# Handing out freed on-chip places in another order between two mixtures of a fused attention and two-mixture kernel

## The chip, the cores and the metric

The kernel runs on one core of one Trainium2 chip. The metric is the device time of one execution in microseconds (us), the median of several runs. Engines are named as the profile names them: PE (TensorE, matrix multiplies), DVE (VectorE), ACT (ScalarE), POOL (GpSimd) and SP (the sync engine, which issues all transfers here).

## The reference

```python
attn_out = _attn_ref(q, k, v)            # 4 x 8 heads x 576 x 64: pooled attention + local attention
x = attn_out.transpose(0, 2, 1, 3).reshape(2304, 512)
# first mixture, d_ff 2048
h = x @ w_in
x = (h * cos(h)) @ w_out
# second mixture, d_ff 1536
xn = x / sqrt(mean(x * x) + 1e-6) * rms_g
g = xn @ w_gate
out = (g * sigmoid(g) * (xn @ w_val)) @ w_out2
```

All is in fp32; the weights of both mixtures arrive as 64-bit words and are turned into fp32 on the chip.

## The kernel before, in words

The tokens are 9 tiles of 256. The first mixture takes tiles 0 to 4 one at a time, then 5 and 6 as a pair, then 7 and 8 as the last pair. For the last pair it walks over 16 slices of d_ff (units 0 to 15). Each unit is one product `h` (line 1004, 12 matmuls, w_in piece) and, once cos has been worked out, one product `y` (line 1070, 12 matmuls, w_out piece) that adds into four PSUM banks. They are called h0 to h15 and y0 to y15 here. Between h and y of a unit stand ACT (lines 1022, 1027, 1038) and DVE (1024, 1029, 1040; 1040 sometimes on POOL). A product in fp32 is made of three passes over a high and a low part, so each operand is split into a rounded part (ACT) and a remainder (DVE or POOL).

The second mixture has 12 weight slices c and three groups g of three token tiles. Its g and val products (line 1499, `gvp`, 36 steps n in the order of the list `CG`; the first steps are c = 0, 1, 2 with g = 0) are done by a seven-product scheme, so weights and tokens first need sums and differences. What each needs:

- A weight slice c: its fp32 pieces are loaded from a scratch array in HBM into a tile `wf` (line 1269, 512 KB), then DVE and POOL form four differences (`wt`, line 1339), ACT rounds (line 1353) and DVE or POOL form remainders (line 1355) into tiles `wc` and `wv`. This is called the split of slice c.
- A token tile t: it is normalised (`norm`: load `y2`, squares, a chain of eleven small DVE instructions on `nst`, a scaling at line 1422 or 1424, transposes `yt` on PE at line 1404), stored (line 1415) and loaded again (`yn`, line 1461); then sums `xs` (line 1468) and remainders `xc` (line 1478). The second half is called the comb of tile t. Tiles 7 and 8 skip the store and load.

All of these tiles live in 19 on-chip places `wa0` to `wa18` of 4 KB per partition. Seventeen of them hold w_in and w_out pieces of the first mixture; each comes free when the last pair has used its piece, and goes to the pool `lt`. The other two carried the second mixture's weights while they were still 64-bit words (staging); they go to the pool `wx` once the last word piece has been written to HBM. The function `late` takes places one after the other and hands them out as `y` (token tiles, two halves of the pair named y and s), `s` (sums, and the differences `wt` of a split), `wf`, or as parts of a weight set `W` (three `wc` and half a `wv`). Since `late` takes them strictly in the order that it lists, a place that is free can stay unused while `late` waits for an earlier one.

The order of instructions on each engine is fixed when the program is built, by a planner (class `Order`, line 55): generators ask for engines and places, and the planner always issues what could start first by its own table of costs. On the chip each engine then runs its list in order, and so does SP's queue of transfers: a transfer that waits for its place holds back all behind it.

```python
    def free_w(p):
        give("lt" if p[2] == "wa" else p[2], p)
```
```python
        yield wait(("wfs", C2 - 1))
        for _ in range(2):
            p = yield take("wa")
            give("wx", p)
```

Of the kernel before, what the change touches and what calls it, by code (L numbers as in the profile page):

```python
# [10 lines left out]
F32R = mybir.dt.float32r  # L11
# [14 lines left out]
NG = 3  # L26
GT, SW = NTILE // NG, TT // 2
C2 = DFF2 // 128
# [26 lines left out]
class Order:  # L55
# [20 lines left out]
    def give(self, name, item, t=None):  # L76
        self.pools.setdefault(name, []).append((self.now() if t is None else t, item))
# [4 lines left out]
    @staticmethod  # L82
    def wait(ev):
        return "wait", ev

    @staticmethod
    def take(name, rest=0):
        return "take", name, rest
# [103 lines left out]
def fused_kernel(ctx: ExitStack, tc, q, k, v, w_in, w_out, w_gate, w_val, w_out2, rms_g, mask, bmask, out):  # L192
# [3 lines left out]
    wait, take, give, done = S_.wait, S_.take, S_.give, S_.set  # L196
# [76 lines left out]
    W, WP = {}, {}  # L273
# [814 lines left out]
    def y_bank(j, y, yi, i, tag, x, t0):  # L1088
# [22 lines left out]
    us = dram.tile([C2, 128, NTILE, 2, SW], F32, name="us")  # L1111
    EARLY = 3
    EN, NE = 5, 4
    LATE1 = ("y", "s", "y", "s", "y", "s")
    LATE2 = ("wf", "wf")
    LATE = C2 - 3
    CG = [(c, g) for g in range(NG) for c in range(EARLY)] + [(c, g) for c in range(EARLY, LATE) for g in range(NG)] \
        + [(c, g) for g in range(NG) for c in range(LATE, C2)]
    SG = ((0, 1), (2, 3), (4, 5), (6, 7), (8,))
    C3 = C2 // 2  # L1120
    YB = (("y", "st"), ("y", "wo"))
# [1 line left out]
    def due2(n):  # L1123
        return T0 + T1 * NTILE + GU * n
# [7 lines left out]
    def second_mixture():  # L1132
# [19 lines left out]
        give("xc", pr.tile([128, 7, 2, 2, GT * SW], F32R, tag="xc0", name="xc"))  # L1152
        done("p2")
        S_.add(late(), 0.0)
        S_.add(w2_loads(), 0.0)
        for t in range(EN, NTILE):
# [18 lines left out]

    def late():
        yield wait("p2")
        for n in LATE1:
            p = yield take("lt")
            give(n, p)  # L1180
        v = []
        for x in range(3):
            w = []
            for _ in range(3):
                p = yield take("lt" if x == 0 else ("lt", "wx"))
                w.append(p[0].tile([128, 2, 4, 128], F32R, tag=p[1], name="wc"))
            if x < 2:
                p = yield take("lt" if x == 0 else ("lt", "wx"))
                v.append(p[0].tile([128, 2, 2, 2, 128], F32R, tag=p[1], name="wv"))
            w.append(v[x // 2][:, x % 2])  # L1190
            give("W", w)
            for n in LATE2 if x == 0 else ():
                p = yield take("lt")
                give(n, p)
    def y_last(j, y, yi):
        due = S_.cur["due"]
        t0 = (S_.cur["t"], "PE")
        ts = xs(T1S[j])[2]
        for t in ts:
            y_i = yield take("y")  # L1200
            s_i = yield take("s")
            st = yield take("nst")
            P2["yr", t] = y_i[0].tile([128, 2, DM], F32, tag=y_i[1], name="y2"), y_i, s_i[0].tile([128, 4, TT], F32, tag=s_i[1], name="yT"), s_i, st
        for i in range(len(yi)):
            S_.add(y_square(ts[i // 2], i % 2, y[i], i, yi[i], t0), due)
            S_.add(y_copy(ts[i // 2], i % 2, y[i], i, yi[i], t0), due)
# [54 lines left out]
    def w2_loads():  # L1261

        for c in range(C2):
            S_.due(due2(CG.index((c, 0))) - 40.0)
            x = yield take("wf")
# [54 lines left out]
    def splits():  # L1320
        for c in range(C2):
            d = due2(CG.index((c, 0))) - 20.0
            S_.due(d)
# [164 lines left out]
    def product(n, m, bank, first, at):  # L1488
        c, g = CG[n]
        x, k, part = MW[m]  # L1490
        yield wait(("sp", c, k))
        S_.due(due2(n) + GU / 7 * at)
        yield "PE", 1.05
        w = P2["W", c][k][:, :, 2 * part:2 * part + 2]
        xc = P2["xc", g]
        i = 0
        for kk in range(2):
            for a, b in ((0, 0), (0, 1), (1, 0)):
                PE.matmul(bank, w[:, a, kk], xc[:, x, b, kk], start=first and i == 0, stop=i == 5, skip_group_check=True)  # L1499
                i += 1  # L1500
# [6 lines left out]
    def products():  # L1507
        N = NG * C2
        for n in range(N + 1):
            d = due2(n) - EV  # L1510
            if n < N:
                c, g = CG[n]
                for j in range(GT):
# [20 lines left out]
            if n:  # L1534
                yield wait(("v2", n - 1))
                yield from product(n - 1, 3, p["e"][1], False, 11)
                S_.add(ev_p1(n - 1, p), d)
                pc, pg = CG[n - 1]
                if pg == NG - 1:
# [12 lines left out]
    def half(x):  # L1552
        return x[:, :GT * SW]
# [44 lines left out]
    def ev_p1(n, st):  # L1598
        yield from ev_add(st["e"][1], st["u2"], st["u2"], None)
        free_bank(st["e"][0])  # L1600
        yield wait(("sl", n))
        yield from ev_u(n, st["u2"], st["sl"], 0)

    def ev_u(n, v, sl, s):
# [3 lines left out]
        yield "SP", 0.6  # L1608
        c, g = CG[n]
        SP.dma_start(us[c, :, GT * g:GT * g + GT, s], half(v).rearrange("p (j w) -> p j w", j=GT))  # L1610
# [234 lines left out]
```

## Time and profile before

| what | value |
|---|---|
| time, median of 3 runs | 992.78 us (992.71 to 993.03) |
| the profiled execution | 994.65 us, of it 992.6 us from the first to the last instruction (the span) |
| PE busy | 956.1 us, 96% of the span |
| PE busy from 200 to 400 us, and from 620 to 900 us | 199.7 of 200 us, 279.9 of 280 us |
| DVE busy | 721.8 us, 73% |
| ACT busy | 543.7 us, 55% |
| POOL busy | 272.6 us, 27% |
| mean granted PE clock | 0.993 of full speed |

A row of a timeline gives the start, the length up to the end of its last instruction, the engine, the source line, the operation, what it writes and reads, and how often; in square brackets stands the idle time before it and what ended that. Since matmuls overlap at their ends, the cost of a group is best read from its start to the start of the next. Windows give the busy time of every engine in a stretch. All times are from the start of the span.

### The profile page before, as it was taken

To read this page: it belongs to the slowest core of one execution; us is meant where nothing else is said; L and a number is where in the kernel's file an instruction comes from. 1 tells how busy PE (TensorE), PEld (TensorE's weight loads), DVE (VectorE), ACT (ScalarE), POOL (GpSimd) and SP (SyncE) were. 2 spreads that over 40 slices of the span, in tenths; PEclk is the share of its full clock that TensorE was granted. 3 is DMA by queue.
4 is the path that set the end of the run, shared out by engine and by line. 5 is a ranking of instruction groups with operands and counts; after the bars stand their busy time and mean duration, and the time that the engine had idled before them with its cause. 6 is when DMAs were issued, how large, how long until landed. Compare 5 with 4: busy or idle time off the path is not lost.

```text
span 992.6 us, 19109 instructions
## 1 busy us (share of the span) xinstructions
PE 956.1 (96%) x7102; PEld 880.5 (89%) x7102; DVE 721.8 (73%) x1459; ACT 543.7 (55%) x1090; POOL 272.6 (27%) x326
## 2 busy tenths in 40 slices
PE   6888899999999999999999989999999999999998
PEld 6787788888988888788888878999999999999998
DVE  2789976587767675666584698587666688999895
ACT  3657985678587865647564555243222334544442
POOL 3867675444435311001050452000000014300000
PEclk9999999999999999999999999999999999999999
DMA  8788634567766653543231311232322144454432
GB/s 236 214 230 250 180 118 118 159 182 194 214 201 171 183 167 118 186 147 143 89 123 43 128 64 32 65 91 81 95 77 77 49 149 133 124 170 138 150 118 75
DMA packets 160333, 136.07 MB, mean 137 GB/s; under 512 B 72176, under 2 KB 133744, under 8 KB 160240
## 3 DMA queue, kind: packets, MB, share of 16 engines
q1 hardware_dynamic: 160240, 134.85, 45.1%
q8 instruction: 56, 0.92, 0.4%
q14 instruction: 37, 0.30, 0.1%
HBM read 98.64 MB, written 36.18 MB: 136 GB/s over the span
## 4 chain that ended last, share of the span: by engine, by line
PE 81%; DVE 6%; issue 3%; POOL 3%; SPq 3%; DMA 2%; ACT 2%; DVEq 0%; POOLq 0%; ACTq 0%
PE gvp L1499 26%; PE y L1070 18%; PE h L1004 17%; PE o L1752 13%; PE bav L745 2%; PE btr L641 1%; SPq L475 1%; PE avp L589 1%; POOL wwa L322 1%; PE yt L1404 1%; DVE xc L1478 1%; PE bs L684 1%; PE bat L720 1%; DMA pq<-in_q 1%; PE sps L534 1%
## 5 line engine op out<-in xcount | busy, mean ns | idle before, releaser
L1499 PE MATMUL gvp<-xc,wc 128*128 128x384 f32 x1296 | 232.9, 336 | 1.5 <-ACT tmp L1561 1.4
L1499 PEld LDWEIGHTS gvp<-xc,wc 128*128 128x128 f32 x1296 | 226.4, 189 | 2.4 <-ACT tmp L1561 1.7
L1570 DVE TENSOR_TENSOR tmp<-gvp,tmp 128x384 f32<-128x384 f32 x180 | 99.5, 554 | 58.1 <-PE gvp L1499 53.7
L1004 PE MATMUL h<-big,wwa 128*128 128x256 f32 (+1 forms) x756 | 125.5, 319 | 1.5 <-DVE t L1029 1.0
L1004 PEld LDWEIGHTS h<-big,wwa 128*128 128x128 f32 x756 | 108.7, 192 | 11.9 <-DVE t L1029 1.2
L1752 PE MATMUL o<-wo,wc 128*128 128x256 f32 x972 | 118.5, 280 | 0.1
L1752 PEld LDWEIGHTS o<-wo,wc 128*128 128x128 f32 x972 | 115.7, 190 | 0.3 <-DVE tmp L1776 0.3
L1070 PE MATMUL y<-wwa,big 128*128 128x512 f32 x432 | 110.0, 398 | 3.6 <-DVE big L1040 3.6
L1070 PEld LDWEIGHTS y<-wwa,big 128*128 128x128 f32 x432 | 78.7, 188 | 21.4 <-DVE big L1040 5.4
L1004 PE MATMUL h<-big,wwb 128*128 128x256 f32 (+1 forms) x504 | 84.8, 319 | 0.1
L1070 PE MATMUL y<-wwb,big 128*128 128x512 f32 x324 | 82.2, 398 | 1.1 <-POOL big L1040 1.1
L1024 DVE SCALAR_TENSOR_TENSOR t<-kk,h 128x512 f32<-128x512 int32 x72 | 48.9, 681 | 43.7 <-ACT kk L1022 43.5
L1004 PEld LDWEIGHTS h<-big,wwb 128*128 128x128 f32 x504 | 72.8, 192 | 7.7 <-issue 0.8
L1022 ACT ACTIVATE kk<-h 128x512 int32<-128x512 f32 x72 | 42.6, 591 | 55.4 <-PE h L1004 55.1
L1070 PEld LDWEIGHTS y<-wwb,big 128*128 128x128 f32 x324 | 59.0, 188 | 13.7 <-POOL big L1040 1.7
L1636 POOL TENSOR_TENSOR wt<-wo 128x256 f32<-128x256 f32 x10 | 9.8, 978 | 208.7 <-DVE wc L1355 183.4
L1029 DVE TENSOR_TENSOR t<-h,t 128x512 f32<-128x512 f32 x72 | 49.3, 686 | 20.0 <-ACT t L1027 19.6
L1038 ACT ACTIVATE big<-t 128x512 fp32r<-128x512 f32 x72 | 45.2, 628 | 29.9 <-DVE t L1029 28.7
L1027 ACT ACTIVATE t<-t,cst 128x512 f32<-128x512 f32 x72 | 51.8, 721 | 17.1 <-DVE t L1024 16.7
L1561 ACT ACTIVATE tmp<-gvp 128x384 f32<-128x384 f32 x36 | 17.7, 491 | 78.1 <-PE gvp L1499 77.9
L1695 ACT ACTIVATE wc<-ut 128x512 fp32r<-128x512 f32 (+1 forms) x60 | 34.2, 584 | 44.2 <-DVE ut L1681 27.5
L1040 DVE TENSOR_TENSOR big<-t,big 128x512 fp32r<-128x512 f32 x56 | 42.9, 767 | 19.0 <-ACT big L1038 18.8
(184 smaller groups left out, 1738.3 us busy)
## 6 DMA issues: line engine op xcount, KB each, us to landing
us<-tmp SPq DMA_DIRECT2D x72, 192.0 KB, 2.0
uf<-us SPq DMA_DIRECT2D x48, 256.0 KB, 2.9
rawwa<-in_moe_w_out SPq DMA_DIRECT2D x21, 512.0 KB, 4.4
wfs<-rawwa SPq DMA_DIRECT2D x36, 256.0 KB, 2.5
rawwa<-in_moe_w_gate SPq DMA_DIRECT2D x12, 512.0 KB, 4.0
rawwa<-in_moe_w_val SPq DMA_DIRECT2D x12, 512.0 KB, 4.6
wf<-wfs SPq DMA_DIRECT2D x12, 512.0 KB, 4.0
vb<-in_v SPq DMA_DIRECT2D x80, 64.0 KB, 2.9
```

What stands on the lines that cost most here:

```text
L1004: PE.matmul(h[:, w_ * ci:w_ * ci + w_], a[:, ksl], x_at(x, kk), start=m == 0, stop=m == 11)
L1022: ACT.activation(out=kk, in_=h, func=ACTF.Copy, scale=INV2PI, bias=0.25)
L1024: DVE.scalar_tensor_tensor(out=t, in0=kk, scalar=TWOPI, in1=h, op0=ALU.mult, op1=ALU.subtract)
L1027: ACT.activation(out=t, in_=t, func=ACTF.Sin, scale=-1.0, bias=cst[:, 0:1])
L1029: DVE.tensor_tensor(out=t, in0=h, in1=t, op=ALU.mult)
L1038: ACT.activation(out=gh, in_=t, func=ACTF.Copy)
L1040: (POOL if e == "POOL" else DVE).tensor_tensor(out=gl, in0=t, in1=gh, op=ALU.subtract)
L1070: PE.matmul(y[j][b], g[:, tsl], a, start=(first and ci == 0 and i == 0), stop=(last and c == 15 and i == 2))
L1499: PE.matmul(bank, w[:, a, kk], xc[:, x, b, kk], start=first and i == 0, stop=i == 5, skip_group_check=True)
L1570: DVE.tensor_tensor(out=half(o), in0=a, in1=half(b), op=ALU.add)
L1695: ACT.activation(out=o[:, 0], in_=src, func=ACTF.Copy)
L1752: PE.matmul(b[m][1][:, l], u[0][x][:, j, l], w[:, y, k], start=(p == 0 and l == 0 and i == 0), stop=(p == C3 - 1 and i == 2), skip_group_c ...
```

## The change

`late` gets one list instead of two. Before: `y s y s y s`, then the weight set of slice 0 with the first `wv`, then two `wf`, then the sets of slices 1 and 2, and all up to the two `wf` came out of `lt` alone. Now: two `wf`, which come out of `wx` alone; then `y s y s`, the first `wv`, the sets of slices 0 and 1, the third `y s`, the second `wv` and the set of slice 2, all out of whichever of the two pools has the place that came free first. The constant `LATE` gets a new meaning and the old one is renamed `GC`. Nothing is computed differently, and every engine has the same instructions but for two or three small ones that move between DVE and POOL; the planner's order changes.

```diff
--- before.py
+++ after.py
@@ -1111,11 +1111,10 @@
     us = dram.tile([C2, 128, NTILE, 2, SW], F32, name="us")
     EARLY = 3
     EN, NE = 5, 4
-    LATE1 = ("y", "s", "y", "s", "y", "s")
-    LATE2 = ("wf", "wf")
-    LATE = C2 - 3
-    CG = [(c, g) for g in range(NG) for c in range(EARLY)] + [(c, g) for c in range(EARLY, LATE) for g in range(NG)] \
-        + [(c, g) for g in range(NG) for c in range(LATE, C2)]
+    LATE = ("wf", "wf", "y", "s", "y", "s", "v", 0, 0, 0, 1, 1, 1, "y", "s", "v", 2, 2, 2)
+    GC = C2 - 3
+    CG = [(c, g) for g in range(NG) for c in range(EARLY)] + [(c, g) for c in range(EARLY, GC) for g in range(NG)] \
+        + [(c, g) for g in range(NG) for c in range(GC, C2)]
     SG = ((0, 1), (2, 3), (4, 5), (6, 7), (8,))
     C3 = C2 // 2
     YB = (("y", "st"), ("y", "wo"))
@@ -1175,23 +1174,18 @@
 
     def late():
         yield wait("p2")
-        for n in LATE1:
-            p = yield take("lt")
-            give(n, p)
-        v = []
-        for x in range(3):
-            w = []
-            for _ in range(3):
-                p = yield take("lt" if x == 0 else ("lt", "wx"))
-                w.append(p[0].tile([128, 2, 4, 128], F32R, tag=p[1], name="wc"))
-            if x < 2:
-                p = yield take("lt" if x == 0 else ("lt", "wx"))
+        v, w = [], {}
+        for n in LATE:
+            p = yield take("wx" if n == "wf" else ("lt", "wx"))
+            if n in ("y", "s", "wf"):
+                give(n, p)
+            elif n == "v":
                 v.append(p[0].tile([128, 2, 2, 2, 128], F32R, tag=p[1], name="wv"))
-            w.append(v[x // 2][:, x % 2])
-            give("W", w)
-            for n in LATE2 if x == 0 else ():
-                p = yield take("lt")
-                give(n, p)
+            else:
+                w.setdefault(n, []).append(p[0].tile([128, 2, 4, 128], F32R, tag=p[1], name="wc"))
+            for n in [n for n in w if len(w[n]) == 3 and len(v) > n // 2]:
+                give("W", w.pop(n) + [v[n // 2][:, n % 2]])
+
     def y_last(j, y, yi):
         due = S_.cur["due"]
         t0 = (S_.cur["t"], "PE")
```

With the new lists the places are these. Before: h11's place (free when h11 has run) and h12's place went to the `wf` of slices 0 and 1. Now these two `wf` lie in the staging places; slice 0's set lies in pieces of units 1, 4 and 2, slice 1's in those of y3, y4 and h11; the third `y` lies in h12's place and the third `s` in y11's.

SP's queue first. `wf_6443` is slice 0's load before, `wf_5921` and `wf_5937` are slices 0 and 1 now, `wf_6271` is slice 2; `yn_6468`, `yn_6470` before and `yn_6505`, `yn_6507`, `yn_6525` now are tiles 3, 4 (and 5) loaded for their combs. Before, around the first weight load:

```order
L1415 DMA xns_102<-yT_6085 128x1024
L1415 DMA xns_102<-yT_6126 128x1024
L1269 DMA wf_6443<-wfs_103 128x1024
L1461 DMA yn_6468<-xns_102 128x1024
L1461 DMA yn_6470<-xns_102 128x1024
L1269 DMA wf_6486<-wfs_103 128x1024
L1461 DMA yn_6471<-xns_102 128x1024
```

Now, from the last early stores on:

```order
L1409 DMA xns_102<-yT_5539 128x1024
L1409 DMA xns_102<-yT_5713 128x1024
L1263 DMA wf_5921<-wfs_103 128x1024
L1263 DMA wf_5937<-wfs_103 128x1024
L1455 DMA yn_5954<-xns_102 128x1024
```

and further down, at the place that the first fence shows of before:

```order
L1409 DMA xns_102<-yT_6126 128x1024
L1263 DMA wf_6271<-wfs_103 128x1024
L1409 DMA xns_102<-yT_6247 128x1024
L1455 DMA yn_6505<-xns_102 128x1024
L1455 DMA yn_6507<-xns_102 128x1024
L1455 DMA yn_6525<-xns_102 128x1024
L1263 DMA wf_6508<-wfs_103 128x1024
L1263 DMA wf_6712<-wfs_103 128x1024
```

The loads of slices 0 and 1 moved from behind the stores of tiles 5 and 6 to ahead of the first token load (`yn_5954` is tile 0); slice 2's now stands ahead of the store of tile 6 and of the loads of tiles 3 to 5.

PE next, from the last h and y units to the first steps of the second mixture. `y_6742`/`y_6744` before and `y_6734`/`y_6736` now are tiles 7 and 8; `h<-big` and `y<-big` without a weight name are units whose weights lie in another buffer (h15, y14, y15). Before, from y12 on:

```order
L1070 MATMUL y<-wwa_1659,big 128x512 x12
L1070 MATMUL y<-wwa_1769,big 128x512 x12
L1004 MATMUL h<-big 128x512 x12
L1070 MATMUL y<-big 128x512 x12
L1499 MATMUL gvp<-xc,wc 128x384 x24
L1070 MATMUL y<-big 128x512 x12
L1499 MATMUL gvp<-xc,wc 128x384 x30
L1499 MATMUL gvp<-xc,wv 128x384 x6
L1404 MATMUL yt<-ident,y_6742 128x128 x8
L1499 MATMUL gvp<-xc,wc 128x384 x6
L1404 MATMUL yt<-ident,y_6744 128x128 x8
L1499 MATMUL gvp<-xc,wc 128x384 x30
```

Now, from y12 on:

```order
L1070 MATMUL y<-wwa_1659,big 128x512 x12
L1004 MATMUL h<-big 128x512 x12
L1070 MATMUL y<-wwa_1769,big 128x512 x12
L1493 MATMUL gvp<-xc,wc 128x384 x6
L1070 MATMUL y<-big 128x512 x12
L1493 MATMUL gvp<-xc,wc 128x384 x12
L1070 MATMUL y<-big 128x512 x12
L1493 MATMUL gvp<-xc,wc 128x384 x36
L1493 MATMUL gvp<-xc,wv 128x384 x6
L1398 MATMUL yt<-ident,y_6734 128x128 x8
L1493 MATMUL gvp<-xc,wc 128x384 x12
L1398 MATMUL yt<-ident,y_6736 128x128 x8
```

h15 now runs ahead of y13, and only 18 of step 0's matmuls stand ahead of y15 where 24 stood. Further up the list (not shown) tile 5's transposes stand behind h6 and those of tile 6 in two halves between y6 and y8; before, both tiles' stood around h6.

DVE last, up to the remainder of h15 (`big` out of `t_6661` before, out of `t_6648` now). `wf_6486` and `wt_6611` are slice 1 and `wf_6535` and `wt_6646` slice 2 before; `wf_6271` and `wt_6664` are slice 2 now. Before, from the remainder of h14 on:

```order
L1040 TENSOR_TENSOR big_93<-t_6584,big_93 128x512
L1339 TENSOR_TENSOR wt_6611<-wf_6486,wt_6611 128x256
L1355 TENSOR_TENSOR wc_6485<-wt_6611,wc_6485 128x512
L1478 TENSOR_TENSOR xc_6454<-xs_6534,xc_6454 128x2x2x128
L1355 TENSOR_TENSOR wc_6528<-wt_6611,wc_6528 128x512
L1339 TENSOR_TENSOR wt_6646<-wf_6535 128x256
L1024 SCALAR_TENSOR_TENSOR t_6661<-kk_6662,h_6567 128x512
L1355 TENSOR_TENSOR wc_6583<-wf_6535,wc_6583 128x512
L1029 TENSOR_TENSOR t_6661<-h_6567,t_6661 128x512
L1355 TENSOR_TENSOR wc_6609<-wt_6646,wc_6609 128x512
L1570 TENSOR_TENSOR tmp_6455<-gvp_6686,tmp_6455 128x384
L1040 TENSOR_TENSOR big_93<-t_6661,big_93 128x512
```

Now, from h14's product with cos on:

```order
L1029 TENSOR_TENSOR t_6601<-h_6553,t_6601 128x512
L1472 TENSOR_TENSOR xc_6491<-yn_6525,xc_6491 128x2x2x128
L1472 TENSOR_TENSOR xc_6491<-xs_6548,xc_6491 128x2x2x128 x2
L1024 SCALAR_TENSOR_TENSOR t_6648<-kk_6649,h_6610 128x512
L1333 TENSOR_TENSOR wt_6664<-wf_6271 128x256
L1333 TENSOR_TENSOR wt_6664<-wf_6271,wt_6664 128x256
L1349 TENSOR_TENSOR wc_6600<-wf_6271,wc_6600 128x512
L1029 TENSOR_TENSOR t_6648<-h_6610,t_6648 128x512
L1349 TENSOR_TENSOR wc_6613<-wt_6664,wc_6613 128x512
L1040 TENSOR_TENSOR big_93<-t_6648,big_93 128x512
L1349 TENSOR_TENSOR wc_6657<-wt_6664,wc_6657 128x512
L1564 TENSOR_TENSOR tmp_6492<-gvp_6683,tmp_6492 128x384
```

Before, parts of two splits and a comb stand between the remainders of h14 and h15; now it is one split and a comb, h14's remainder has gone to POOL, and the split of slice 1 stands some 25 rows further up, between h10 and h12 (slice 0's still further, between h4 and h7).

## Rows read from the trace of the kernel before

**Rows 1.** Windows of 20 us: busy us (instructions) of each engine, clock, DMA share, GB/s.
```profile
core 0: us, PE busy (x) PEld busy (x) DVE busy (x) ACT busy (x) POOL busy (x), PEclk, DMA share, GB/s
...
500.00:520.00 20.00, 20.00 (x90) 16.57 (x89) 18.30 (x35) 14.20 (x32) 11.18 (x12) 1.00 0.32 107
...
540.00:560.00 20.00, 20.00 (x90) 16.57 (x89) 9.07 (x14) 8.00 (x13) 1.84 (x2) 1.00 0.23 78
560.00:580.00 20.00, 17.35 (x74) 13.39 (x74) 20.00 (x25) 12.70 (x25) 17.49 (x17) 1.00 0.24 81
580.00:600.00 20.00, 17.73 (x94) 15.71 (x93) 17.00 (x41) 12.98 (x28) 8.33 (x11) 1.00 0.23 80
600.00:620.00 20.00, 18.34 (x98) 17.83 (x97) 17.76 (x36) 11.16 (x25) 3.07 (x4) 0.91 0.13 39
```

**Rows 2.** TensorE in order of time: start us, us, what, idle before and its releaser.
```profile
516.77 2.88 PE L1004 MATMUL h<-big,wwb 128*128 128x512 f32 x12
...
567.52 3.46 PE L1070 MATMUL y<-wwa,big 128*128 128x512 f32 x13
572.87 2.79 PE L1070 MATMUL y<-wwa,big 128*128 128x512 f32 x11 [1.89 <-DVE big L1040]
575.50 2.88 PE L1004 MATMUL h<-big 128*128 128x512 f32 x12
578.22 0.39 PE L1070 MATMUL y<-big 128*128 128x512 f32 x1
...
588.24 2.88 PE L1070 MATMUL y<-big 128*128 128x512 f32 x12
590.96 5.46 PE L1499 MATMUL gvp<-xc,wc 128*128 128x384 f32 x30
...
597.96 0.33 PE L1404 MATMUL yt<-ident,y 128*128 128x128 f32 x1 [0.48 <-ACT y L1422]
...
602.03 0.33 PE L1404 MATMUL yt<-ident,y 128*128 128x128 f32 x1 [1.41 <-ACT y L1422]
...
603.94 6.49 PE L1499 MATMUL gvp<-xc,wc 128*128 128x384 f32 x30
...
611.32 6.42 PE L1499 MATMUL gvp<-xc,wc 128*128 128x384 f32 x36
...
618.62 6.41 PE L1499 MATMUL gvp<-xc,wc 128*128 128x384 f32 x36
```

**Rows 3.** Chain that ended last, one piece: start us, us, what.
```profile
522.38 0.87 PE yt L1404 x8
```

**Rows 4.** Sync engine's queue of transfers, in order of time.
```profile
554.12 0.32 SPq L1269 DMA_DIRECT2D wf<-wfs  x1
554.54 1.03 SPq L1461 DMA_DIRECT2D yn<-xns  x2
```

**Rows 5.** VectorE by shape, 470 to 500 us: busy us, mean ns.
```profile
L1040 DVE TENSOR_TENSOR big<-t,big 128x512 fp32r<-128x512 f32 x5 | 3.5, 693 | 2.9 <-ACT big L1038 2.8
```

**Rows 6.** The same view, 557 to 589 us.
```profile
L1040 DVE TENSOR_TENSOR big<-t,big 128x512 fp32r<-128x512 f32 x5 | 5.0, 1002 | 0.0
L1478 DVE TENSOR_TENSOR xc<-xs,xc 128x512 fp32r<-128x512 f32 x4 | 3.2, 814 | 0.0
L1478 DVE TENSOR_TENSOR xc<-yn,xc 128x512 fp32r<-128x512 f32 x3 | 3.1, 1041 | 0.0
...
L1029 DVE TENSOR_TENSOR t<-h,t 128x512 f32<-128x512 f32 x4 | 2.7, 681 | 0.0
```

**Rows 7.** GpSimd by shape, 557 to 590 us: busy us, mean ns.
```profile
L1478 POOL TENSOR_TENSOR xc<-xs,xc 128x512 fp32r<-128x512 f32 x2 | 3.5, 1730 | 0.0
```

**Rows 8.** TensorE alone in short windows: busy us (instructions), granted clock, DMA share, GB/s.
```profile
570.00:573.00 3.00, 1.11 (x6) 1.00 0.00 0
...
600.00:602.00 2.00, 0.62 (x4) 1.00 0.00 0
...
604.00:607.00 3.00, 3.00 (x14) 0.64 0.01 2
```

## The prediction

> **What bounds the kernel now.** I read the windows first. PE has no gap to speak of from 200 us to 900 us but in one place: in 540 to 560 us it is busy all 20 us, in 560 to 580, 580 to 600 and 600 to 620 only 17.35, 17.73 and 18.34 us, the last with the granted clock down to 0.91 [rows 1]. This is the passage from the first mixture to the second. In the same 560 to 580 DVE is busy 20.00 of 20 us, and POOL, which did 1.84 us in the window before, 17.49; but from 540 to 560 DVE has 9.07 us of work [rows 1]. So DVE idles just before the stretch in which it holds everything up.
>
> The PE timeline gives what the passage costs. A unit of the first mixture takes 2.72 us from start to start (575.50 to 578.22), a step of 42 second-mixture matmuls 7.30 us (611.32 to 618.62), that is 0.174 us each [rows 2]; a set of eight transposes takes 0.87 us [rows 3]. From 567.52 to 590.96 us PE ran y12, y13, h15, y14, y15 and 24 matmuls of step 0: 5 x 2.72 + 24 x 0.174 = 17.8 us of work in 23.44 us, so 5.7 us lost. One of its waits stands in a row: y13 stopped for 1.89 us for a remainder of line 1040 on DVE [rows 2]. From 590.96 to 611.32 it ran 78 such matmuls and two sets of transposes, 13.6 + 1.7 = 15.3 us in 20.36, so 5.1 us lost: the transposes of tile 7 (597.96) and tile 8 (602.03, after 1.41 us) waited for ACT's scaling at line 1422 [rows 2], and after that idling the clock fell, 0.64 granted in 604 to 607 us [rows 8]. At 2.4 GHz the 36 matmuls from 603.94 to 611.32 would take 6.3 us and took 7.4 [rows 2], so 1.1 us of the 5.1 is clock. In all the passage loses 10.7 us; nothing else on PE waits after it, so what is saved here reaches the end whole.
>
> Why is DVE idle before 557 us? Since the weights of slice 0 were not there: SP issued the load at 554.12 us, when h11 had set its place free, and the loads of tiles 3 and 4 stood behind it in SP's queue and left at 554.54 [rows 4]. Splits of three slices and combs of three tiles then fell together with the remainders of h12 to h15.
>
> **The change part by part.** *The two weight loads.* They now lie in places that have long been free, and on SP stand right behind the early stores. 1 MB moves out of the passage to before 500 us. It is hidden behind units that need no transfer; with DMA engines at a share of 0.32 in 500 to 520 [rows 1] I cost it at nothing.
>
> *Slice 0's split* moves from 557 us to behind h4 and h5, where its set is complete (the last place is y2's). There DVE was already busy 18.30 of 20 us [rows 1], so this is not free room. The split's part on DVE is four remainders, of 0.69 us with POOL idle [rows 5] or about 1.0 with POOL busy [rows 6]: 2.8 to 4.1 us. On the other side tile 6's norm leaves this place, and only one of the four stands ahead of h4's remainder. PE gives more room than before: y5 now has h6, tile 5's transposes and h7 ahead of it. I take no stall; the bound if the cover is gone is 4.1 us.
>
> *Tile 6's norm* comes later, since only two y/s pairs exist then; its transposes stand ahead of y7 and y8. PE starts h5 at 516.77 [rows 2]; seven units and tile 5's transposes later (19.0 + 0.9) it reaches them at 536.7. The norm waits for h7's work on DVE, which ends some 3 us after h7 (528.5), then needs the chain on `nst` and one scaling: about 535. I take no stall.
>
> *Slice 1's split* needs h11's place. With 12 units and two sets of transposes after 516.77, h11 ends at 551.2. Its work falls into 551 to 558 us, DVE's half idle window. No stall.
>
> *The tight stretch.* Eight units on, without stalls, PE is at y13 at 572.9; y14 follows after one unit and 6 matmuls at 576.7, y15 after one unit and 12 matmuls at 581.5. h12 ends at 559.3 and, with 0.7 us for ACT's conversion (taken as DVE's 0.69 for the shape [rows 5]), DVE begins its line 1024 at 560.0. From there to h15's remainder its list has 29 instructions: 8 with an operand in PSUM at 0.68 us, 14 of 512 columns at 0.81 to 1.04 us, of which I take 0.9 [rows 6], and 7 of half the size at half of that: 5.4 + 12.6 + 3.2 = 21.2 us, so 581.2 against 581.5. With 0.69 [rows 5] for the 14 and half for the 7 it is 577.6, with 1.04 [rows 6] 583.7: 3.9 early to 2.2 late. h13's remainder (7, 5 and 5 of them) comes at 572.0 against 572.9. h14's is now POOL's: its product with cos ends at 573.5, then 0.7 for ACT and 1.73 on POOL [rows 7] make 575.9 against 576.7. All three hold by under 1 us, and some DVE instructions will wait for ACT, so I take 0.7 us of stall where 5.7 were lost.
>
> Rows and a rule meet here. The same remainder of line 1040 takes 693 ns where POOL is idle and 1002 ns where it is busy [rows 5, 6], while line 1029, with an operand in PSUM, stays at 681 [rows 6]. The Trainium skill says the same (GPSIMD Engine Reference, "8. Key points"): POOL shares its SBUF interfaces with VectorE, in contention with DVE instructions that have two SBUF inputs. It speaks against this change, since POOL's work goes along with DVE's to the new places, slice 0's into a stretch where DVE is already full. By the rule the sum would stand at its late end, 2.2 us, and the trace bears it out so far.
>
> *Behind y15* (ends at 584.2). Before, tile 7's transposes could start 7.0 us after y15's end (590.96 to 597.96) and tile 8's 11.1 us after it (602.03) [rows 2]. Now 42 matmuls, 7.3 us, stand between y15 and the first: covered. PE asks for the second after 7.3 + 0.9 + 12 x 0.174 = 10.3 us: 0.8 late by the old pace. But tile 8's `nst` chain now stands on DVE ahead of the sum that waits for m3, so it starts earlier. Bounds 0 and 0.8; I take 0.5. With so little idling the clock should stay up; 1.1 us if it falls as before.
>
> Sum: 10.7 - 0.7 - 0.5 = 9.5 us. The profiled execution's 994.65 us (span 992.6) would become 985.1; it lay 1.87 us over the median, and the median of 992.78 becomes **983.3 us**.
>
> **The rivals.** *VectorE stays the bound.* All shared work runs at the slow price, 2.2 us at y15, the overfull place at h4 and h5 costs up to 4.1 us, the old pace at tile 8 0.8 us and the clock 1.1 us. For it: the 18.30 us [rows 1] and the rule above; against it: the whole saved room in 540 to 560. Loss 3 to 8 instead of 1.2, so 985.5 to 990.
>
> *Nothing gained.* The new order waits as long in other places: the 24 instructions of two splits (four differences, roundings and remainders each) are gone from the passage, but slice 2's set still needs y13's place, and the third token pair comes only with h12 and y11, so combs 3 to 5 stay. If these, not the splits, set the pace, 991 to 994.6. Against it: the passage holds one split where three stood.
>
> *Slower.* Tile 6's transposes stand in PE's list ahead of y7, y8 and all behind. Each us that their scaling comes after 536.7 is lost. It needs the load of the tile, which waits for comb 2's place, two squares on ACT behind h6's and h7's work, the chain and the scaling. It decides from 9.5 us late, at 546.2; 12 us late would give 995.3. Against it: the load can leave once comb 2 is done, which falls at the end of DVE's full window (520) [rows 1], 16 us ahead.
>
> *The clock.* The Trainium skill (TensorE: Matmul & The Clock Gate, Part 1) has PE fall to half clock after idling. The rows agree only in part: 1.00 was granted in 570 to 573 with 1.11 of 3 us busy, 0.64 in 604 to 607 after 600 to 602 with 0.62 of 2 [rows 8]; it is a price inside the first rival, not one by itself.
>
> **How the numbers follow.** The forecast, 982 to 985.5, has 0.63; VectorE as the bound 0.24; nothing gained 0.07; slower 0.06. No change can be told from 0.2% (2.0 us). Faster by more: the first two and a little of the third, 0.88; same 0.06; slower 0.06. If no loss is left the time is 982.1; I let the range begin at 981.8 and take in most of the first rival, up to 988.8.
>
> **What would show it.** Right: SP loads slice 0 and 1 before 500 us; DVE splits slice 0 near 515 to 528 and slice 1 near 551 to 558; PE waits under 1 us at y13, y14, y15; y15 ends near 584 us; tile 8's transposes wait under 1 us; no clock below 1.00 at 595 to 610; some 9 us less at the first full step. Wrong: PE idle at y4, y5 or ahead of tile 6's transposes near 537 (rival one or three), or DVE without a gap from 551 to 590.

## The result and the profile after

The changed kernel takes 984.91 us (median, 982.76 to 986.51), the kernel before 992.82 us beside it: a ratio of 0.9918, 95% interval 0.9906 to 0.9931. That is 7.9 us faster, where 9.5 were forecast; the predicted 983.3 us lies 1.6 us too low. The profiled execution took 986.51 us, of it a span of 984.7 us, in which PE was busy for 954.6 us (97%). Two later series of the same kernel gave medians of 984.4 and 984.05 us beside 992.69 and 992.87 us.

The windows of the changed kernel, with the same columns as in [rows 1]:

```profile
core 0: us, PE busy (x) PEld busy (x) DVE busy (x) ACT busy (x) POOL busy (x), PEclk, DMA share, GB/s
...
500.00:520.00 20.00, 20.00 (x90) 16.58 (x89) 16.79 (x25) 14.13 (x28) 12.34 (x14) 1.00 0.29 98
520.00:540.00 20.00, 20.00 (x96) 16.65 (x95) 15.80 (x37) 13.36 (x27) 4.67 (x6) 1.00 0.21 77
540.00:560.00 20.00, 20.00 (x92) 16.57 (x91) 10.40 (x17) 7.80 (x14) 2.82 (x4) 1.00 0.23 79
560.00:580.00 20.00, 20.00 (x92) 16.73 (x91) 18.57 (x28) 13.87 (x27) 10.88 (x11) 1.00 0.15 54
580.00:600.00 20.00, 18.98 (x110) 17.95 (x109) 17.20 (x43) 14.55 (x33) 7.79 (x8) 1.00 0.21 73
600.00:620.00 20.00, 20.00 (x116) 20.00 (x115) 16.73 (x33) 7.31 (x16) 1.65 (x2) 1.00 0.17 50
```

The PE column is the result: 20.00 in 560 to 580 and in 600 to 620, where [rows 1] has 17.35 and 18.34, and a granted clock of 1.00 in place of 0.91. DVE did as much work in 560 to 580 as before, all but 1.4 us, and POOL 10.88 us in place of 17.49; PE no longer waits for DVE there.

PE in order of time, changed kernel, as [rows 2]:

```profile
517.86 2.88 PE L1004 MATMUL h<-big,wwb 128*128 128x512 f32 x12
...
537.81 0.60 PE L1398 MATMUL yt<-ident,y 128*128 128x128 f32 x4
...
552.37 5.60 PE L1070 MATMUL y<-wwb,big 128*128 128x512 f32 x24
...
574.13 2.88 PE L1070 MATMUL y<-wwa,big 128*128 128x512 f32 x12
...
577.91 2.88 PE L1070 MATMUL y<-big 128*128 128x512 f32 x12
...
582.75 2.88 PE L1070 MATMUL y<-big 128*128 128x512 f32 x12
585.47 6.53 PE L1493 MATMUL gvp<-xc,wc 128*128 128x384 f32 x36
...
597.09 1.09 PE L1398 MATMUL yt<-ident,y 128*128 128x128 f32 x8 [1.02 <-DVE y L1418]
...
603.32 6.47 PE L1493 MATMUL gvp<-xc,wc 128*128 128x384 f32 x36
```

y13 (574.13), y14 (577.91) and y15 (582.75) start without a bracket, so without a wait; the only wait between 480 and 640 us is 1.02 us at tile 8's transposes. From h5's start to the point at which 102 second-mixture matmuls have been issued, PE now needs 603.32 - 517.86 = 85.46 us; before it was 611.32 - 516.77 = 94.55 us [rows 2]. I call this the passage. It gave 9.1 us, and what lies behind it took as long in both traces (381.3 and 381.4 us to the end of the span). That is more than the medians show, since h5 itself starts 1.09 us later in this trace than in the one of before, though all engines have the same lists up to about 480 us.

### The profile page after: what moved, and what is told of

The parts are those of the page before. It is cut to its first block, busy times and chain, and to the rows that moved or that the text cites. A ratio compares the mean times of both kernels' runs of the same rounds, so it can differ in the third digit from the quotient of the medians.

```text
span 984.7 us, 19115 instructions
## 1 busy us (share of the span) xinstructions
PE 954.6 (97%) x7102; PEld 881.4 (90%) x7102; DVE 724.0 (74%) x1460; ACT 542.8 (55%) x1090; POOL 268.5 (27%) x325
## 4 chain that ended last, share of the span: by engine, by line
PE 83%; POOL 4%; DVE 3%; SPq 3%; issue 3%; DMA 2%; ACT 2%; DVEq 0%; POOLq 0%; ACTq 0%
PE gvp L1493 26%; PE y L1070 19%; PE h L1004 18%; PE o L1746 13%; PE bav L745 2%; PE btr L641 1%; SPq L475 1%; POOL wwa L322 1%; DMA v<-in_v 1%; SPq L807 1%; PE avp L589 1%; PE bs L684 1%; PE yt L1398 1%; PE bat L720 1%; SPq L478 1%
## 5 line engine op out<-in xcount | busy, mean ns | idle before, releaser
L1038 ACT ACTIVATE big<-t 128x512 fp32r<-128x512 f32 x72 | 45.2, 629 | 25.0 <-DVE t L1029 23.6
L1040 DVE TENSOR_TENSOR big<-t,big 128x512 fp32r<-128x512 f32 x54 | 40.0, 741 | 16.5 <-ACT big L1038 16.2
```

Source lines behind the costliest of these rows:

```text
L1038: ACT.activation(out=gh, in_=t, func=ACTF.Copy)
L1040: (POOL if e == "POOL" else DVE).tensor_tensor(out=gl, in0=t, in1=gh, op=ALU.subtract)
```

## The experiments

The first table holds for all of them. "Lost" is worked out as in the prediction: from h5's start to y15's end less 23 units of 2.72 us, two sets of transposes of 0.87 and the early matmuls of 0.174; behind y15 the rest of the 102 matmuls and two more sets.

| kernel | median us | passage us | lost up to y15's end | lost behind it |
|---|---|---|---|---|
| before | 992.8 | 94.55 | 5.7 | 5.1 |
| before, second trace | | 94.97 | 6.2 | 5.0 |
| changed | 984.9 | 85.46 | 0.2 | 1.5 |
| changed, second and third trace | 984.4, 984.05 | 85.48, 85.49 | 0.2 | 1.5 |
| early loads, old order | 989.8 | 90.84 | 4.6 | 2.4 |
| order alone | 986.8 | 88.36 | 3.2 | 1.4 |
| before, slice 0 twice | 996.3 | 96.47 | 9.2 | 3.5 |
| changed, slice 0 twice | 987.2, 985.2 | 85.53, 85.54 | 0.3 | 1.4 |
| changed, slice 2 three times | 988.6 | 88.05 | 2.4 | 1.9 |
| changed, tile 6's comb off POOL | 984.25 | 85.16 | 0.2 | 1.2 |
| and tile 8's scaling on ACT | 984.3 | 85.13 | 0.2 | 1.2 |

**Is the early loss the change's?** The changed kernel once more, unaltered.

> The changed kernel once more, unaltered, for a second trace. The first trace of it lost about 1.1 us against the kernel before ahead of 480 us, where both programs are the same (h5 starts at 517.86 against 516.77), and 1.0 us at tile 8's transposes. Theory that the early loss is chance of that execution (when loads land, which clock is granted): h5's start differs by over 0.5 us from 517.86 in this trace, while the passage from h5's start to the 102nd matmul of the second mixture again takes 85.5 us to within 0.5. Theory that the change itself costs 1.1 us early: h5 starts at 517.9 to within 0.3 again. The median by either: 983 to 986 us.

Ratio 0.9916 (0.99 to 0.9933). h5 and the end of the passage in this trace:

```profile
515.68 2.88 PE L1004 MATMUL h<-big,wwb 128*128 128x512 f32 x12
...
601.16 6.42 PE L1493 MATMUL gvp<-xc,wc 128*128 128x384 f32 x36
```

The passage takes 85.48 us, as before to 0.02; h5 starts 2.2 us earlier than in the first trace. The early 1.1 us was chance of that execution.

**The loads alone.**

```diff
-    LATE = ("wf", "wf", "y", "s", "y", "s", "v", 0, 0, 0, 1, 1, 1, "y", "s", "v", 2, 2, 2)
+    LATE = ("wf", "wf", "y", "s", "y", "s", "y", "s", 0, 0, 0, "v", 1, 1, 1, "v", 2, 2, 2)
```

> The early weight loads alone: the two loads go into the first mixture's wide places, but all three y/s pairs still come ahead of slice 0's places, as before the change. Slice 0's set is then complete early, slice 1's only with h13's place. Theory that a slice's split must have both, its load and its set, ahead of the tight stretch: one of three splits leaves the tight stretch instead of two, so about half of the 9 us comes, 987 to 989.5 us, and vector-engine remainders again hold PE up near y13 to y15 for some 2 to 4 us. Rival, the loads are all that counts: 985 us as with the whole change. Rival, the order of the places is all that counts: 992.8 us.

Ratio 0.9967 (0.9956 to 0.9977), 989.77 us. In the passage the loads bring 3.7 us of the 9.1, a little less than half. Two of its PE rows:

```profile
579.30 2.79 PE L1070 MATMUL y<-big 128*128 128x512 f32 x11 [1.51 <-DVE big L1040]
...
602.04 1.09 PE L1398 MATMUL yt<-ident,y 128*128 128x128 f32 x8 [1.35 <-DVE y L1418]
```

A y unit (y14) still waits for its remainder of line 1040, and tile 8's transposes wait nearly as long as in [rows 2]. Both rivals fall. The first theory comes nearest, with a time 0.3 us over its range and one such wait of 1.51 us where 2 to 4 us were expected, but this run does not show its reason. Only 1.1 us of the 3.7 were gained up to y15's end, where slice 0's split has left the stretch. The other 2.6 lie behind it, where PE's list changed too (30 matmuls of step 0 ahead of y15 in place of 24, and 12 in place of 6 between the two sets of transposes) and the granted clock stayed at 1.00.

**The order alone.**

```diff
-    LATE = ("wf", "wf", "y", "s", "y", "s", "v", 0, 0, 0, 1, 1, 1, "y", "s", "v", 2, 2, 2)
+    LATE = ("y", "s", "y", "s", "v", 0, 0, 0, 1, 1, "wf", "wf", 1, "y", "s", "v", 2, 2, 2)
...
-        for n in LATE:
-            p = yield take("wx" if n == "wf" else ("lt", "wx"))
+        for i, n in enumerate(LATE):
+            p = yield take("lt" if i < 12 else ("lt", "wx"))
```

> The order of the places alone: the sets of slices 0 and 1 and only two y/s pairs come first, but the two weight loads go into the places of h11 and h12 (about 551 and 559 us), as late as before the change. Theory that a split needs its load and its set early: both splits stay late, 990 to 993 us, and PE again loses 6 us or more between y12 and the first whole step. Rival, order is what counts (the third y/s pair kept combs out of the way): 985 to 987 us.

Ratio 0.994 (0.9923 to 0.9956), 986.77 us. My theory falls: with loads as late as before, the order alone brings 6.2 of the 9.1 us. PE's waits for line 1040 are there, but short:

```profile
569.57 2.79 PE L1070 MATMUL y<-wwa,big 128*128 128x512 f32 x11 [0.52 <-DVE big L1040]
...
576.12 2.79 PE L1070 MATMUL y<-wwa,big 128*128 128x512 f32 x11 [0.81 <-DVE big L1040]
...
584.71 2.83 PE L1070 MATMUL y<-big 128*128 128x512 f32 x11 [0.73 <-DVE big L1040]
```

What had I missed? The planner's other lists, which change with the order. Slice 0's split starts when its load has come into h11's place: on DVE at 557.68 us before (40.9 us behind h5), here at 556.09 (38.3 behind h5). The place is the same, but PE's list has h11 one unit earlier. Slice 1's differences are formed from 564.34 us on instead of 574.15, and h14's remainder goes to POOL. h15's remainder then ends 66.8 us behind h5, in the kernel before 70.9, in the changed one 63.4. Behind y15, PE's list has 42 matmuls ahead of tile 7's transposes and 12 between the two sets, where it had 36 and 6: 1.4 us lost in place of 5.1. These are readings of the rows; which of the moves is worth how much was not tried apart. The rival named the right time, but its cause is not seen: tiles 3 and 4 are loaded for their combs 35.1 us behind h5, before 37.8, so these combs stay in the stretch.

One more wait of the kernel before went with the order. In the midst of step 0 PE waited for ACT's copy of its first sum, and that copy (585.15 us) stood in ACT's list behind line 1027 of h15, which waited for DVE. PE and ACT, kernel before:

```profile
585.67 2.72 PE L1499 MATMUL gvp<-xc,wc 128*128 128x384 f32 x12 [1.41 <-ACT tmp L1561]
```
```profile
584.00 0.72 ACT L1027 ACTIVATE t<-t,cst 128x512 f32<-128x512 f32 x1 [1.28 <-DVE t L1024]
```

With the early loads alone this wait is still there (1.37 us); with the order alone and in the changed kernel, where fewer matmuls of step 0 stand ahead of y15, it is gone.

In the whole passage loads and order seem to add up: 3.7 + 6.2 = 9.9 us against 9.1 together. Taken apart they do not. Up to y15's end they give 1.1 and 2.6 us alone and 5.5 together, so there it takes both, as the prediction had it; behind y15 they give 2.6 and 3.6 alone and 3.6 together.

**Does DVE hold PE up?** In the kernel before, slice 0's remainders on DVE are written twice.

```diff
         (POOL if e == "POOL" else DVE).tensor_tensor(out=lo, in0=src, in1=hi, op=ALU.subtract)
+        if e == "DVE" and c in (0,):
+            DVE.tensor_tensor(out=lo, in0=src, in1=hi, op=ALU.subtract)
```

> The kernel before, with the vector engine's remainders of slice 0 done twice over (the same values written twice; three or four more instructions of about 0.7 to 1.0 us, inside the tight stretch, nothing else moved). Theory that the vector engine without a gap from 560 to 590 us is what holds PE up there: the time grows by 2 to 4 us, to 995 to 997 us. Rival, the matrix engine waits there for places, loads or combs, and the vector engine is only busy meanwhile: no change, 992.8 us to within 1.

Ratio 1.0035 (1.0021 to 1.0049), 996.25 us: 3.6 us for four more rows of 1.11, 0.69, 1.11 and 0.83 us. Up to y15's end 3.5 us are lost on top, so nearly every us that DVE has more to do there is one that PE comes later: y13 goes on 59.5 us behind h5, before 56.1, and DVE's remainder releases it again. Three of PE's rows, and a window of this kernel:

```profile
569.85 0.50 PE L1070 MATMUL y<-wwa,big 128*128 128x512 f32 x1 [1.97 <-ACT big L1038]
571.59 4.52 PE L1070 MATMUL y<-wwa,big 128*128 128x512 f32 x12 [1.24 <-DVE big L1040]
576.50 2.79 PE L1070 MATMUL y<-wwa,big 128*128 128x512 f32 x11 [0.39 <-DVE big L1040]
```
```profile
570.00:573.00 3.00, 1.76 (x4) 1.19 (x5) 3.00 (x6) 3.00 (x7) 2.80 (x3) 0.73 0.40 153
```

Here the clock falls at the first stall, and not at tile 8's transposes, where the 1.43 us wait comes again (605.67 us). The passage grew by only 1.9 us, just under the 2 of the theory, since behind y15 it got 1.5 back; where the rest of the median's 3.6 lies, the one trace does not show. Of the 1.5, 0.9 can be placed: the 36 matmuls behind the transposes take 6.45 us at full clock and 7.38 before [rows 2]. That is near the 1.1 us clock term of the sum.

**Is slice 0's new place overfull?** The same doubling in the changed kernel.

> The changed kernel, with the vector engine's four remainders of slice 0 (at 515 to 529 us) done twice over, the same values written twice: 3 x 0.68 + 0.42, or 2.5 us more of vector-engine work where the prediction feared an overfull place. Theory that this place has room (no row of the matrix engine waits there, and the vector engine idles 7.4 of the 40 us from 500 to 540): the time does not change, 984.4 us to within 1, and PE still waits for nothing from h4 to tile 6's transposes. Rival, the place is full and only just holds: 1 to 2.5 us more, with a wait at a y unit or at tile 6's transposes.

Ratio 0.9936 (0.9917 to 0.9955), 987.2 us: over the theory's bound. But the passage took 85.53 us, PE waited at tile 8 alone (1.07 us), and h5 started at 518.72 us. So it was run again, beside the changed kernel:

> The run with slice 0's remainders done twice over, once more, beside the changed kernel in the same call. Its first median was 987.2 us, 2.3 to 2.8 over the changed kernel's, while its passage took 85.53 us as without the doubling and its profile was late only ahead of 480 us, where nothing is changed. Theory that this was chance of the early part: the median comes to within 1 us of the changed kernel's in this call, and the passage is 85.5 us again. Rival, the doubling costs 2 us that the one profile did not show: 986.5 us or more, against 984.5 for the changed kernel.

> The changed kernel a third time, to stand beside the run before it: 984 to 985 us, a passage of 85.5 us, and h5's start anywhere from 515 to 518.5 us if the early part varies by chance.

985.18 us (0.9912 to 0.9939) beside 984.05 us (0.9901 to 0.9929), passages 85.54 and 85.49. The medians are 1.1 us apart, a tenth over the bound that I had set, with intervals that overlap; the passage says 0.05. In the one execution of the first series that was traced, the excess lay in the early part: its h5 started 3.3 us later than in the changed kernel's third trace, and its span was 3.3 us longer. The medians alone leave room for a cost of about 1 us; by the passages the place has room for 2.5 us more, and the fear of a 4.1 us cost there was unfounded.

**How near is DVE's bound now?** Slice 2's remainders on DVE done three times over in the changed kernel.

```diff
+        for _ in range(2 if e == "DVE" and c == 2 else 0):
+            DVE.tensor_tensor(out=lo, in0=src, in1=hi, op=ALU.subtract)
```

> The changed kernel, with the vector engine's remainders of slice 2 (three, at 578.6, 579.8 and 581.2 us) done three times over, the same values written: two of them stand ahead of h15's remainder, 4 x 0.6 = 2.4 us more ahead of it. In the trace that remainder ends at 581.2 and y15 is reached at 582.75, 1.5 us later. Theory that the gain came from getting the vector engine's list ahead of that remainder short enough, with some 1.5 us to spare: PE waits about 0.9 us at y15 for that remainder, and the tail behind it comes no more than 1 us later still; 985 to 986.5 us. Rival, the vector engine is far from the bound now: no change, 984.4 us to within 0.5. Rival, it is at the edge already, so each added us costs one: 986.8 us or more.

Ratio 0.9956 (0.9942 to 0.997), 988.61 us. PE at y15:

```profile
583.40 2.81 PE L1070 MATMUL y<-big 128*128 128x512 f32 x11 [1.90 <-DVE big L1040]
```

The place is the one foretold, the size was not: 0.9 expected, 1.90 came. Two of the added rows took 0.92 us in the mean, with POOL busy beside the first, and the remainder itself took 1.21 beside POOL, so DVE's list ahead of it took 23.6 us instead of 19.9, 3.7 more and not 2.4. Of 3.7 us some 1.5 to 1.8 were absorbed, as the theory has it; at the edge nothing would have been. The median rose by about 4 us, which is the second rival's number (986.8 or more), and the profiled passage by 2.6; what the other 1.5 are, the one profile does not show. So the 1.5 us to spare are read from the trace, not from the median.

**POOL beside tile 8's chain.** Changed kernel, DVE and POOL in order of time:

```profile
594.11 1.19 DVE L1380 SCALAR_TENSOR_TENSOR nst<-nst 128x2 f32<-128x2 f32 x1
```
```profile
593.98 1.30 POOL L1472 TENSOR_TENSOR xc<-yn,xc 128x512 fp32r<-128x512 f32 x1 [3.55 <-ACT xc L1470]
```

An instruction on two columns ends at 595.30, just when POOL's on 512 ends (595.28). Its like in the same chain take 0.16 us.

```diff
-        (POOL if e == "POOL" else DVE).tensor_tensor(out=lo, in0=src, in1=hi, op=ALU.subtract)
+        (POOL if e == "POOL" and t != 6 else DVE).tensor_tensor(out=lo, in0=src, in1=hi, op=ALU.subtract)
```

> The changed kernel, with the three remainders of tile 6's comb that POOL does at 593.98, 595.75 and 597.04 us done by the vector engine at the same places of the order, which leaves POOL idle beside tile 8's chain on the vector engine. There one instruction of the chain, on 2 columns, took 1.19 us (594.11, in POOL's 1.30 us from 593.98) where its like take 0.16. Theory that POOL's instruction holds up the vector engine's beside it: that row falls to 0.16 us, the second scaling of tile 8 ends some 0.3 us sooner (1.0 saved, one remainder of about 0.7 more ahead of it), and PE's wait at tile 8's transposes falls from 1.0 to about 0.7; the time is 984.1 us, no change that can be measured. Rival, the long row is a wait of its own (the read of ACT's sums, a semaphore): it stays at about 1.2 us, and the wait at the transposes grows to 1.7.

984.25 us, ratio 0.9911 (0.9896 to 0.9926). The same row of the chain, and PE's wait:

```profile
592.36 0.16 DVE L1380 SCALAR_TENSOR_TENSOR nst<-nst 128x2 f32<-128x2 f32 x1
```
```profile
594.90 1.09 PE L1398 MATMUL yt<-ident,y 128*128 128x128 f32 x8 [0.60 <-DVE y L1418]
```

0.16 in place of 1.19, and the wait falls to 0.60 (0.7 foretold). The hold was POOL's doing. It agrees with the Trainium skill (GPSIMD Engine Reference, "8. Key points"): POOL shares its SBUF interfaces with VectorE.

**The second scaling on ACT as well.**

```diff
-        if e == "ACT":
+        if e == "ACT" or t == 8:
```

> As the run before it (tile 6's comb off POOL), and the second scaling of tile 8 moved from the vector engine, where it stands behind sums of the products, to ACT right behind the first. Theory that the last 1.0 us of waiting in the passage is this scaling's place in the vector engine's list: PE waits 0.3 us or less at tile 8's transposes, the passage from h5's start to the 102nd matmul of the second mixture takes 84.5 us instead of 85.5, and the median is 983.4 to 984 us. Rival, the transposes then wait for ACT instead, as in the kernel before (1.41 us for line 1422): no gain, 984.4 us.

984.31 us, ratio 0.9913 (0.9898 to 0.9929). PE at tile 8:

```profile
594.11 0.33 PE L1398 MATMUL yt<-ident,y 128*128 128x128 f32 x1 [0.29 <-ACT y L1416]
594.72 0.98 PE L1398 MATMUL yt<-ident,y 128*128 128x128 f32 x7 [0.28 <-ACT y L1416]
```

0.57 us of waiting in all, as in the run before it: the wait went from DVE to ACT, as the rival has it, 84.5 us was not reached (85.13), and neither kernel beats the changed one by what can be measured.

**Does the passage of before repeat?** The kernel before once more.

> The kernel before once more, unaltered, for a second trace of it. Theory that the passage is settled by the program and only the part ahead of 480 us varies: from h5's start to the 102nd matmul of the second mixture 94.5 us to within 0.5 again, while h5's start itself may lie anywhere from 515 to 518 us. Rival, the passage varies as much as the whole (the chain's clock drop at 604 us, or a stall at y13, comes and goes): 93.5 us or less, or 95.5 or more.

```profile
520.29 2.88 PE L1004 MATMUL h<-big,wwb 128*128 128x512 f32 x12
...
615.26 6.42 PE L1499 MATMUL gvp<-xc,wc 128*128 128x384 f32 x36
```

94.97 us, within the bound, with the same waits at y13's and y14's remainders (1.85 and 0.71 us), in step 0 and at the transposes, and 0.44 us more at y12's. h5's start lies outside the 515 to 518 us that were expected. This execution took 998.52 us, and all that it is longer lies ahead of h5 (520.29) but for 0.4.

## Why the prediction came out as it did

It was right in direction, in size to 1.6 us, and in its mechanism up to y15; behind y15 one step was wrong. Point by point, with times counted from h5's start, which differs from trace to trace:

- *The two loads.* Foretold before 500 us; SP issued both from 481.28 us on. Costed at nothing, and no row contradicts it.
- *Slice 0's split.* On DVE from 515.41 to 529.45 us, PE waits nowhere: right, and shown by the doubled run. Its remainders cost 2.4 us, under the range of 2.8 to 4.1: one of the four is half as wide, and POOL stood still beside all of them, so the slow price never applied.
- *Tile 6's norm.* Foretold: PE reaches the transposes 19.9 us behind h5; it was 19.95 (537.81). But the scaling ended 19.2 us behind h5 and not some 18, since two instructions of the chain took 1.20 and 0.66 us beside a remainder and a difference of POOL (from 533.77 and 535.02 us). The rival that put the loss here was 0.7 us from starting, not 1.7.
- *Slice 1's split.* h11 ended 34.5 us behind h5 (34.4 foretold), and the split, but for one difference that POOL forms at 535.0, lies in 552.6 to 557.8 us, in DVE's idle stretch: right.
- *The tight stretch.* PE came to y15 64.9 us behind h5, foretold 64.7; h15's remainder ended 63.4 behind it, foretold 64.4. So there was 1.5 us to spare where I had 0.3, and no stall where I took 0.7. Why the list was short: the prices per row were right, and so was the count of 29: they add up to 21.4 us, foretold 21.2. But the stretch, from 561.36 to 581.24 us, is 19.9 us long: in the trace a row of 0.68 us is followed by the next one 0.60 us after its start (572.08, 572.68, 573.28), so rows without a gap overlap, and their sum is some 1.5 us too long. The next view has DVE's rows by shape from 560 to 582 us: busy us, mean ns, idle time before.

```profile
L1472 DVE TENSOR_TENSOR xc<-xs,xc 128x512 fp32r<-128x512 f32 x6 | 5.6, 954 | 0.0
L1472 DVE TENSOR_TENSOR xc<-yn,xc 128x512 fp32r<-128x512 f32 x3 | 3.0, 992 | 0.0
...
L1040 DVE TENSOR_TENSOR big<-t,big 128x512 fp32r<-128x512 f32 x3 | 2.6, 864 | 0.1
```

  They are about as slow as in [rows 6], so the price beside POOL held; it did not decide, since PE had enough work ahead. Of the 5.7 us that the kernel before lost up to y15, the prediction named one wait (1.89 at y13); 1.41 in step 0 and 0.70 at y14 stand in rows too.
- *Behind y15.* This is the step that was mis-sized: "I take 0.5" at tile 8's transposes, with bounds of 0 and 0.8. 1.02 us came, also just over the 1 us that was named as a sign. The reason for going below 0.8, that tile 8's chain "starts earlier", did not come true. DVE before and in the changed kernel:

```profile
597.51 0.56 DVE L1570 TENSOR_TENSOR tmp<-gvp,tmp 128x384 f32<-128x384 f32 x1 [1.25 <-PE gvp L1499]
597.99 0.16 DVE L1383 TENSOR_SCALAR nst<-nst 128x2 f32<-128x2 f32 x1
...
599.56 1.27 DVE L1386 SCALAR_TENSOR_TENSOR nst<-nst 128x2 f32<-128x2 f32 x1
```
```profile
592.54 0.16 DVE L1377 TENSOR_SCALAR nst<-nst 128x2 f32<-128x2 f32 x1
...
596.54 0.49 DVE L1418 TENSOR_SCALAR y<-y,nst 128x512 f32<-128x512 f32 x1
```

  The chain started 7.03 us behind y15's end before (597.99) and 7.07 now (592.54), and DVE's scaling, which the transposes wait for, ended 11.6 us behind it in both. The sum that had waited 1.25 us for PE is gone from ahead of the chain. But tile 7's chain, which stands ahead of it too and starts 1.8 us behind y15 in both, now took 3.97 us (587.26 to 591.23) in place of 2.57 (592.76 to 595.33), with four sums of POOL beside it (587.47 to 590.43) where POOL was idle before up to 594.59. So POOL took back what the order gave; this is a reading of the rows. In tile 8's own chain POOL held one row up in both kernels (1.27 us before, 1.19 now); without that hold the wait was 0.60, as the run with tile 6's comb off POOL shows. Another 0.5 us lies in small gaps between transposes and matmuls. So 1.7 us of the 10.7 were left, and not 1.2: 0.2 up to y15 where I took 0.7, and 1.5 behind it where I took 0.5. The two errors partly cancel.
- *The clock* stayed at 1.00, as foretold.
- *From the passage to the median.* Here the prediction assumed that the part ahead of the passage is the same in both. Of the 9.1 us, the three series show 7.9, 8.3 and 8.8. The lists there are the same, the traces of one kernel differ by up to 3.5 us in it, and chance can explain the gap; whether all of it is chance stays open.

Of the reasons, one was incomplete: I put the gain down to two splits that leave the stretch. The order alone, with both loads late, gives 6.2 of the 9.1 us, 3.6 of them behind y15 where no split is worked on; up to y15 it gives 2.6 of 5.5. The prediction read the new PE list and used it for its times, but did not ask what it was worth by itself. Of the rivals, "VectorE stays the bound" fell; in the kernel before it was the bound (slice 0 twice), and the changed one is 1.5 us from it (slice 2 three times).

## What to carry to other kernels

Where one engine is idle just before the stretch in which it holds up another, look for what keeps its work from starting: here the order in which freed places were handed out, and the loads and other engines' lists that hang on it. When an order changes, test it apart from the transfers it was meant for. Measure such a change from an instruction ahead of it to one behind it in the trace, since the rest of a run can vary by a good part of the gain (here by up to 3.5 us, against 9.1); and where a queue runs without gaps, add up starts, not row lengths.

## What the hardware showed beyond that

- A DVE instruction on two columns lasted as long as the POOL instruction beside it: 1.19 us in place of 0.16, back at 0.16 with POOL idle.
- With the same lists up to 480 us, h5 started at 515.42 to 518.72 us in the traces of the changed kernel and of those made from it, and at 516.77 and 520.29 in two of the kernel before. The passage repeated within 0.03 and 0.4 us.
- The granted clock after a stall does not follow from how little PE did: it fell to 0.64 at 604 us in the kernel before [rows 8] and to 0.65 in its second trace (means of stretches that lay partly at 1.2 and partly at 2.4 GHz; 603 to 605 us in the kernel before shows 0.50, all at 1.2), behind 2 us with 0.62 and 0.59 us of PE work; with 0.69 us in 2 (early loads, old order, 600 to 602) and with 0.56 in 2 (before, slice 0 twice, 604 to 606) it stayed at 1.00. The Trainium skill (TensorE: Matmul & The Clock Gate, Part 1) has PE fall to half clock after idling; these rows agree in part, as those of the prediction did.
